# Attention of the later tiles with 64 and 8 keys of a head computed apart

## The chip, the cores and the metric

The kernel runs on one NeuronCore of one Trainium2 chip. The metric is device time in microseconds for one execution. The engines are named as the profile names them: PE (TensorE, matmuls) and PEld (its weight loads), DVE (VectorE), ACT (ScalarE), POOL (GpSimd) and SP (SyncE, which here only issues DMAs). Each engine works through its own list of instructions in order, and waits for the others through semaphores.

## The reference

Attention over keys and values that are averaged in groups of eight, followed by a two-layer network:

```python
B, H, S, D = 8, 8, 576, 64          # Sp = 576 // 8 = 72 pooled keys a head
k_p = k.reshape(B, H, Sp, 8, D).mean(axis=3)
v_p = v.reshape(B, H, Sp, 8, D).mean(axis=3)
scores = (1 / sqrt(D)) * q @ k_p.T   # per batch and head: 576 x 72
attn = softmax(scores)
x = (attn @ v_p)  -> (B*S, H*D) = (4608, 512)
h = x @ w_in      # 512 x 2048
out = (h * sigmoid(h)) @ w_out       # 2048 x 512
```

Inputs and outputs are float32; the products run in bfloat16 with float32 sums.

## The kernel before

The 4608 tokens are cut into nine tiles of 512. While the network's matmuls of tile t run, the attention of tile t + 1 is fitted in between. The network is computed by a seven-product scheme on halves (`unit`, line 678, and `out_product`, line 647), so that sums of inputs (`unit_x_sum`, line 476) and of hidden blocks (`hidden_sum`, line 574) stand ahead of the products.

The order on every engine is written out by hand. `tile_products` (line 615) walks through a string of items such as `a1` or `P5`; each is some steps long, 112 in an ordinary tile. A list of fillers is attached to step numbers by `at` and `late`, and `spread` (line 426) emits a filler behind its step. A filler's matmuls thus go between the network's, and its work on the other engines goes to the end of those engines' lists at that moment. Two fillers on the same engine run in the order of their steps.

Attention of one tile, for tiles 1 to 8, has these parts.

- Keys: `k_transpose` (line 202) or, for the first batches, `select_k` and `copy_k` put the pooled keys of batch b in `kz[b % 2]`. Four heads of 32 value pairs each lie on the 128 partitions (a is the group of four heads, c the even or odd half of D).
- Scores: `scores` (line 350) does one half of the tile's tokens (256) in one visit, at step 63 and again at 78. For each of four heads and two groups a matmul of 32 rows by 72 keys runs on its own quarter of the rows of PE. ACT takes the exponential of four 72 x 512 blocks (line 356).
- Sums: `denominators` (line 358) multiplies by ones, 72 rows by 32 columns, four column quarters; `reciprocals` (line 370) follows as exp(-ln).
- Values: `numerators` (line 401), 72 rows by 32 columns, into two banks a half; `x_half` (line 410) multiplies by the reciprocals on DVE and writes `xT`.

A tile that spans two batches has its matmuls cut in two at the border.

PSUM has eight banks: three go round under the tag `mm`, five under `at`. A tile takes the next in the round, so it waits for whoever used that bank last.

POOL's list in tile t, for t from 2 on: `behind_x_sums` (line 481), which copies one number of the last x sum and so waits for it; `pool_k` (line 194) for batch t + 1; the load of the next batch's first half of k (`load_one`, line 176); `pool_v` (line 197); the first half of v; the second halves (`load_rest`, line 182), which add onto the first halves and so wait until these have landed; and `load_q` at step 33. In tile 1 the loads come without the pooling, since batch 2 is pooled elsewhere. In tile 5 `load_q` consists of eight DMAs, since it is the last batch's; in tile 6 nothing is left to load.

The start is a stretch of its own: POOL issues the first loads of q and v, sets `shifts` and the identity, and then issues the loads of `w_in` (line 788).

Of the kernel before, what the change touches and what calls it, by code (L numbers as in the profile page):

```python
# [27 lines left out]
FP32 = mybir.dt.float32  # L28
# [8 lines left out]
def kernel(  # L37
# [62 lines left out]
    ones = singles.tile([SP, 32], BF16, name="ones")  # L100
# [18 lines left out]
    kz = [singles.tile([128, 2, 2, SP], BF16, name=f"kz{n}") for n in range(2)]  # L119
    kp = singles.tile([128, H, D], BF16, name="kp")  # L120
# [44 lines left out]
    PH = POOL // 2 * D  # L165

# [9 lines left out]
    def load_one(b, name):  # L176
        st = batches.setdefault(b, {})
        raw = raw_tile(f"{name}_raw3", H)
        nc.gpsimd.dma_start(out=raw, in_=source(b, name)[:, :, :PH])
        st[f"{name}_raw"] = raw  # L180

    def load_rest(b, name):
        nc.gpsimd.dma_start(
            out=batches[b][f"{name}_raw"], in_=source(b, name)[:, :, PH:],
            accum_op=ALU.add,
        )
# [9 lines left out]

    def pool_v(b):
        st = batches[b]
        st["vp"] = mid.tile([SP, H, D], BF16, tag="vp", name="vp")
        pool_rows(st["vp"], st["v_raw"])  # L200
# [91 lines left out]
    def select_v(b, a, tag="at"):  # L292
        st = batches[b]
        if a == 0:
            st["v_ps"] = ps_tile([128, H, D], FP32, tag, "v_ps")
            st["vp"] = mid.tile([SP, H, D], BF16, tag="vp", name="vp")
# [8 lines left out]

    def copy_v(b, a, copy=nc.vector.tensor_copy, heads=4):
        hs = slice(4 * a, 4 * a + heads)
        copy(out=batches[b]["vp"][:, hs, :], in_=batches[b]["v_ps"][:SP, hs, :])
# [14 lines left out]
    def es_tile():  # L323
        return mid.tile([SP, 4, 2 * NQ], BF16, tag="es", name="es")
# [25 lines left out]
    def scores(t, f):  # L350
        sc = [ps_tile([128, 512], FP32, "at", "sc_ps")[:SP] for s in range(4)]
        for g in range(2):
            score_matmuls(sc, t, f, g, g * NQ)
        es = half_state(t, f)["es"] = es_tile()
        for s in range(4):
            nc.scalar.activation(es[:, s, :], sc[s], func=AF.Exp, scale=score_scale)  # L356

    def denominators(t, f, den_ps=None):
# [3 lines left out]
        for s in range(4):  # L362
            nc.tensor.matmul(  # L363
                den_ps[32 * s : 32 * (s + 1), :],
                lhsT=ones, rhs=st["es"][:, s, :], start=True, stop=True,
            )
# [8 lines left out]
    def numerator_matmuls(nu, t, f, g, c, c0):  # L375
        for b, _, cs in half_units(t, f):
            for s in range(4):
                nc.tensor.matmul(  # L378
                    nu[32 * s : 32 * (s + 1), c0 + cs.start : c0 + cs.stop],
                    lhsT=batches[b]["vp"][:, 4 * g + s, c::2],  # L380
# [20 lines left out]
    def numerators(t, f, tags=("at", "at")):  # L401
        st = half_state(t, f)
        nu = []
        for c in range(2):
            nu.append(ps_tile([128, 512], FP32, tags[c], "nu_ps"))
            for g in range(2):
                numerator_matmuls(nu[c], t, f, g, c, g * NQ)
        st["nu"] = nu

    def x_half(t, f):  # L410
        st = half_state(t, f)
        for c in range(2):
            nc.vector.tensor_mul(  # L413
                out=xT[:, c::2, x_cols(t, f)],
                in0=st["nu"][c].rearrange("r (g n) -> r g n", g=2),
                in1=st["rec"].rearrange("r (g n) -> r g n", g=2),
            )
# [363 lines left out]
    nc.vector.memset(kp, 0.0)  # L781
    nc.gpsimd.memset(shifts, 0.0)
    make_identity(nc, ident, nomemset=True)

# [76 lines left out]
    for n in range(4):  # L861
        unit_weight_sum(0, 1, n)
    denominators(0, 1, den_ps)
# [28 lines left out]
    for t in range(NT):  # L892
        a = t + 1
        if t == 0:
# [17 lines left out]
            for j in range(2):  # L912
                at(60 + 2 * j, select_k, 1, j)
                at(60 + 2 * j, copy_k, 1, j, nc.scalar.copy)
            for i0, i1 in ((0, SA), (SA, SLOTS), (SLOTS, SLOTS + 1)):
                at(55, load_slots, nc.gpsimd, 2, "k", i0, i1)
# [8 lines left out]
            for j in range(2):  # L925
                at(83 + j, slot_sums, "v", j)
                at(100 + j, select_v, 1, j)
            at(101, copy_v, 1, 0, nc.scalar.copy, H)
# [5 lines left out]
            at(68, scores, 1, 0)  # L934
            at(79, scores, 1, 1)
            at(79, denominators, 1, 0)
            at(94, reciprocals, 1, 0)
            at(103, denominators, 1, 1)
            at(103, reciprocals, 1, 1)
            at(106, numerators, 1, 0)  # L940
            at(106, numerators, 1, 1, ("at", "mm"))
            for n in range(2):
                at(106, x_half, 1, n)
# [27 lines left out]
        if a < B:  # L971
            if t == 1:
                for j in range(2):
# [3 lines left out]
                    at(69, slot_sums, "v", j, halves=True)  # L977
                at(1, load_half_2, "v", 1)
                for j in range(2):
                    at(84, select_v, 2, j)  # L980
                at(84, copy_v, 2, 0, nc.scalar.copy, H)
# [5 lines left out]
            else:  # L987
# [10 lines left out]
                at(34, k_transpose, a)  # L998
        if t < NT - 1:
# [6 lines left out]
            late(63, scores, a, 0)  # L1006
            late(78, scores, a, 1)
            late(89, denominators, a, 0)
            late(89, reciprocals, a, 0)
            late(89, denominators, a, 1)  # L1010
            late(89, reciprocals, a, 1)
            for n in range(2):
                late(89, numerators, a, n)
            late(89, x_half, a, 0)
            late(91, moe_tables)
            late(95, x_half, a, 1)
# [32 lines left out]
```

## Time and profile before

| | |
|---|---|
| median of 3 runs | 273.1 us (272.92 to 273.17) |
| profiled execution: span | 272.3 us |
| ACT, exponential of the scores (line 356) | 64 x 590 ns |
| DVE, values times reciprocals (line 413) | 32 x 683 ns |
| POOL, pooling of k and v (lines 189 and 192) | 10 x 2357 ns, 10 x 1266 ns |
| POOL waiting for x sums (line 482) | 41.7 us in 6 waits |
| POOL waiting for the first half of v (line 183) | 14.6 us in 5 waits |
| POOL waiting for the first half of k (line 183) | 9.9 us in 5 waits |
| DMA | 37.72 MB, 139 GB/s mean |

The span runs from the first to the last instruction of the profiled execution; the measured time has a little more around it. A row of a timeline gives the start and the length in microseconds, the engine, the line of the kernel, the operation, what it writes and reads, its shape and how many follow each other; a bracket names the idle time before it and what ended it. Matmuls are pipelined: the length of one has its way through the array in it, and the distance from start to start is what a stream of them costs.

### The profile page before, as it was taken

To read this page: it belongs to the slowest core of one execution; us is meant where nothing else is said; L and a number is where in the kernel's file an instruction comes from. 1 tells how busy PE (TensorE), PEld (TensorE's weight loads), DVE (VectorE), ACT (ScalarE), POOL (GpSimd) and SP (SyncE) were. 2 spreads that over 40 slices of the span, in tenths; PEclk is the share of its full clock that TensorE was granted. 3 is DMA by queue.
4 is the path that set the end of the run, shared out by engine and by line. 5 is a ranking of instruction groups with operands and counts; after the bars stand their busy time and mean duration, and the time that the engine had idled before them with its cause. 6 is when DMAs were issued, how large, how long until landed. Compare 5 with 4: busy or idle time off the path is not lost.

```text
span 272.3 us, 7297 instructions
## 1 busy us (share of the span) xinstructions
PE 266.3 (98%) x2982; PEld 213.9 (79%) x2982; DVE 206.5 (76%) x363; ACT 194.1 (71%) x342; POOL 102.3 (38%) x111
## 2 busy tenths in 40 slices
PE   8999999999999999999999999999999999999994
PEld 4358644788888878887888788878888888788883
DVE  4759886879697949794979497849875987587861
ACT  1579776888858885888588858785878587867700
POOL 8655435672348413831383329383800000000000
PEclk9999999999999999999999999999999999999999
DMA  7999999586996796679657976799400140014004
GB/s 214 269 203 281 216 289 304 177 150 156 133 200 168 148 137 150 157 148 147 132 140 164 125 154 164 155 130 123 126 2 2 40 117 1 2 34 120 4 2 154
DMA packets 31585, 37.72 MB, mean 139 GB/s; under 512 B 10640, under 2 KB 22608, under 8 KB 31552
## 3 DMA queue, kind: packets, MB, share of 16 engines
q0 software_dynamic: 23904, 26.64, 52.4%
q1 hardware_dynamic: 7216, 9.97, 13.3%
q10 hardware_dynamic: 432, 0.66, 0.7%
q8 instruction: 23, 0.38, 0.6%
q14 instruction: 10, 0.08, 0.1%
HBM read 36.70 MB, written 9.44 MB: 169 GB/s over the span
## 4 chain that ended last, share of the span: by engine, by line
PE 92%; DMA 6%; POOL 0%; issue 0%; DVE 0%; POOLq 0%
PE u_psB L636 17%; PE o_psB L655 16%; PE u_psA L636 11%; PE u_psE L636 11%; PE o_psA L655 11%; PE o_psE L655 10%; PE o_ps L553 5%; PE sc_ps L331 3%; DMA raw<-in_v_dram 3%; DMA w_in_sb<-in_moe_w_in_dram 3%; PE nu_ps L378 3%; PE hp_ps L525 2%; PE den_ps L363 2%; POOL q_bf L127 0%; PE kz_ps L283 0%
## 5 line engine op out<-in xcount | busy, mean ns | idle before, releaser
L636 PEld LDWEIGHTS <-w_sum 128*128 128x128 bf16 x544 | 52.8, 98 | 7.5 <-issue 1.0
L655 PEld LDWEIGHTS <-h_sum 128*128 128x128 bf16 x512 | 48.6, 98 | 9.1 <-issue 2.6
L636 PEld LDWEIGHTS <-w_in_sb 128*128 128x128 bf16 x408 | 39.9, 98 | 5.0 <-issue 0.2
L655 PEld LDWEIGHTS <-h_T 128*128 128x128 bf16 x384 | 36.9, 98 | 5.3 <-issue 1.0
L636 PE MATMUL u_psA<-xT,w_in_sb 128*128 128x256 bf16 x272 | 40.5, 273 | 0.0
L636 PE MATMUL u_psB<-x_sum,w_sum 128*128 128x256 bf16 x272 | 40.2, 272 | 0.0
L356 ACT ACTIVATE es<-sc_ps 72x512 bf16<-72x512 f32 x64 | 32.7, 590 | 2.8 <-PE sc_ps L331 1.9
L655 PE MATMUL o_psB<-w_sum,h_sum 128*128 128x256 bf16 x256 | 33.0, 273 | 0.0
L655 PE MATMUL o_psA<-w_out_sb,h_T 128*128 128x256 bf16 x256 | 32.1, 273 | 0.0
L670 DVE TENSOR_TENSOR u_psE<-u_psB,p 128x512 f32<-128x512 f32 x34 | 23.7, 697 | 10.0 <-ACT p L668 6.1
L413 DVE TENSOR_TENSOR xT<-nu_ps,rec 128x512 bf16<-128x512 f32 x32 | 20.4, 683 | 12.6 <-ACT rec L373 10.5
L674 ACT ACTIVATE h_T<-u_psE 128x512 bf16<-128x512 f32 x34 | 20.3, 597 | 11.2 <-PE u_psE L636 10.4
L687 DVE TENSOR_TENSOR c<-u_psB,p 128x512 f32<-128x512 f32 x34 | 23.2, 681 | 3.1 <-PE u_psB L636 2.1
L665 DVE COPY u_psB<-u_psA 128x512 f32<-128x512 f32 x30 | 20.9, 698 | 5.5 <-PE u_psA L636 3.8
L674 ACT ACTIVATE h_T<-u_psB 128x512 bf16<-128x512 f32 x34 | 20.4, 599 | 5.9 <-PE u_psB L636 5.9
L674 ACT ACTIVATE h_T<-u_psA 128x512 bf16<-128x512 f32 x34 | 20.5, 602 | 4.7 <-PE u_psA L636 4.5
L189 POOL TENSOR_TENSOR raw<-raw 72x1024 f32<-72x1024 f32 x10 | 23.6, 2357 | 0.1
L668 ACT COPY p<-u_psE 128x512 f32<-128x512 f32 x34 | 20.0, 593 | 4.2 <-PE u_psE L636 4.0
L579 DVE TENSOR_TENSOR h_sum<-h_T 128x1024 bf16<-128x1024 bf16 x32 | 21.7, 680 | 0.2 <-ACT h_T L674 0.2
L674 ACT ACTIVATE h_T<-c 128x512 bf16<-128x512 f32 x34 | 21.7, 637 | 0.0
L579 DVE TENSOR_TENSOR h_sum<-h_T,h_sum 128x1024 bf16<-128x1024 bf16 (+1 forms) x24 | 20.7, 864 | 0.2
L636 PE MATMUL u_psB<-xT,w_sum 128*128 128x256 bf16 x136 | 20.6, 272 | 0.0
(89 smaller groups left out, 438.7 us busy)
## 6 DMA issues: line engine op xcount, KB each, us to landing
out_dram<-o_sb SPq DMA_DIRECT2D x128, 64.0 KB, 1.7
raw<-in_k_dram POOLq DMA_DIRECT2D x10, 576.0 KB, 8.2
raw<-in_v_dram POOLq DMA_DIRECT2D x10, 576.0 KB, 8.6
q_bf<-in_q_dram POOLq DMA_DIRECT2D x5, 576.0 KB, 11.3
w_in_sb<-in_moe_w_in_dram POOLq DMA_DIRECT2D x8, 256.0 KB, 8.6
w_out_sb<-in_moe_w_out_dram POOLq DMA_DIRECT2D x4, 512.0 KB, 10.7
raw<-in_v_dram POOLq DMA_DIRECT2D x2, 768.0 KB, 10.4
raw<-in_k_dram POOLq DMA_DIRECT2D x2, 768.0 KB, 10.0
```

The costliest lines, as they stand in the source:

```text
L189: nc.gpsimd.tensor_add(out=raw[:, :, : 2 * D], in0=raw[:, :, : 2 * D], in1=raw[:, :, 2 * D :])
L356: nc.scalar.activation(es[:, s, :], sc[s], func=AF.Exp, scale=score_scale)
L413: nc.vector.tensor_mul(out=xT[:, c::2, x_cols(t, f)], in0=st["nu"][c].rearrange("r (g n) -> r g n", g=2), in1=st["rec"].rearrange("r (g n) ...
L553: nc.tensor.matmul(ps["m", m], lhsT=h_T[:, g, m * 128 : (m + 1) * 128], rhs=w_out_sb[:, g, :], start=(g == 0), stop=(g == KG - 1),)
L579: nc.vector.tensor_tensor(out=h_sum[n][:, k0:k1, :], in0=get(a), in1=get(b), op=op)
L636: nc.tensor.matmul(ps[y, BANK[n]][:, u, :], lhsT=w[:, kk, 128 * u : 128 * (u + 1)], rhs=x[:, kk, :], start=n in (1, 5) and u == 0 and kk == 0,
L655: nc.tensor.matmul(o_bank(n, c), lhsT=left(n, kt, c), rhs=w[:, kt, :], start=n in (1, 5) and kt == 0 and c == 0, stop=kt == KQ - 1, skip_g ...
L665: (acopy if t == 0 or (t == 1 and y in (0, 1)) else vcopy)(ps[y, "B"], ps[y, "A"])
L668: acopy(f32[y], ps[y, "E"])
L670: tt(out=ps[y, "E"], in0=ps[y, "B"], in1=f32[y], op=add)
L674: nc.scalar.activation(h_T[:, g : g + 2, j * NQ : (j + 1) * NQ], src, func=AF.Silu)
L687: tt(out=c22, in0=ps[y, "B"], in1=f32[y], op=add)
```

## The change

From tile 1 on, the 72 keys of a head are treated as 64 and 8. `scores(t)` handles the whole tile in one visit: the first 64 keys of the heads of both groups on tiles of 32 rows by 64 columns, eight at a time, with 512 columns each; the last eight keys of four heads go together in one matmul of 128 rows by 32 columns, whose weights `kzr` are block-diagonal (four heads by eight keys, zero elsewhere). The exponentials then are four of 128 x 512 and one of 128 x 256. `sum_matmuls` and `value_matmuls` use tiles of 64 rows by 32 columns for the 64 keys, and add the last eight keys by masked ones `ones_r` and block-diagonal values `vr`.

`spread_keys` makes `kzr` by four products of the last eight keys with a mask, `spread_values` makes `vr` by two; both on POOL unless told otherwise. The values lie in a tile of 128 partitions with a fifth column block for the last keys. For batches 0, 1 and 2 `pick_v` builds it by matmuls (batch 0 also keeps the old form `vp0` for tile 0); for later ones v is loaded in that layout: the first 64 keys in two DMAs for each half, the last eight keys in four DMAs from SP. `pool_v` gets three more additions and calls `spread_values`. Masks are made at the start.

```diff
     def load_one(b, name):
+        if name == "v":
+            st["v_raw"] = big.tile([128, 4, PH], FP32, tag="v_raw3", name="v_raw")
+            st["r_raw"] = big.tile([128, 2 * PH], FP32, tag="r_raw3", name="r_raw")
+            load_v_half(b, 0)
+            for n in range(4):
+                hs = slice(4 * (n // 2), 4 * (n // 2) + 4)
+                nc.sync.dma_start(
+                    out=st["r_raw"][32 * n : 32 * (n + 1)],
+                    in_=v[b].rearrange("h (sp p) d -> h sp (p d)", p=POOL)[hs, KM:],
+                )
+            return
...
+    def load_v_half(b, half):
+        for g in range(2):
+            nc.gpsimd.dma_start(
+                out=batches[b]["v_raw"][KM * g : KM * (g + 1)],
+                in_=source(b, "v")[:KM, 4 * g : 4 * (g + 1), PH * half : PH * (half + 1)],
+                **(dict(accum_op=ALU.add) if half else {}),
+            )
...
     def pool_v(b):
         st = batches[b]
-        st["vp"] = mid.tile([SP, H, D], BF16, tag="vp", name="vp")
-        pool_rows(st["vp"], st["v_raw"])
+        vp = value_tile(b)
+        pool_rows(vp[:, :4], st["v_raw"])
+        raw = st["r_raw"]
+        for w in (PH, PH // 2, PH // 4):
+            nc.gpsimd.tensor_add(
+                out=vp[:, 4] if w == D else raw[:, :w], in0=raw[:, :w], in1=raw[:, w : 2 * w]
+            )
+        spread_values(b)
...
+    def spread_keys(b, eng=nc.gpsimd):
+        for a in range(2):
+            for c in range(2):
+                eng.tensor_tensor(
+                    out=kzr[b % 2][:, a, c].rearrange("r (s k) -> r s k", s=4),
+                    in0=kz[b % 2][:, a, c : c + 1, KM:].broadcast_to([128, 4, SP - KM]),
+                    in1=mask_k.unsqueeze(2).broadcast_to([128, 4, SP - KM]), op=ALU.mult,
+                )
...
+    def pick_v(b):
...
+        for g in range(2):
+            for s in range(4):
...
+                    nc.tensor.matmul(
+                        ps[KM * g : KM * (g + 1), s, :], lhsT=shifts[:, x : x + KM],
+                        rhs=v5[:, i], start=(s == 0 and j == 0), stop=(j == len(segs) - 1),
+                        skip_group_check=True,
+                    )
+        for n in range(4):
+            for s in range(4):
+                h = 4 * (n // 2) + s
+                nc.tensor.matmul(
+                    ps[32 * n : 32 * (n + 1), 4, :], lhsT=pick_r[:, h],
+                    rhs=v5[:, (SP * h + KM) // 128], start=False, stop=(s == 3),
+                    skip_group_check=True,
+                )
+        nc.scalar.copy(value_tile(b), ps)
...
+    def scores(t):
+        st = att[t] = {}
+        sc = [ps_tile([128, 512], FP32, "at", "sc_ps") for _ in range(4)]
+        scr = ps_tile([128, 512], FP32, "at", "sr_ps")
+        for n, (b, us, cs) in enumerate(tile_units(t)):
+            for c in range(2):
+                for s in range(4):
+                    rows = slice(32 * s, 32 * (s + 1))
+                    for g in range(2):
+                        nc.tensor.matmul(
+                            sc[s][KM * g : KM * (g + 1), cs],
+                            lhsT=kz[b % 2][rows, g, c, :KM],
+                            rhs=qT[rows, g, us, :, c],
+                            start=(n == 0 and c == 0), stop=(c == 1), skip_group_check=True,
+                        )
         for c in range(2):
...
+                nc.tensor.matmul(
+                    scr[32 * n : 32 * (n + 1), cs],
+                    lhsT=kzr[b % 2][:, g, c, :], rhs=qT[:, g, us, :, c],
+                    start=(first and c == 0), stop=(c == 1), skip_group_check=True,
+                )
+        for s in range(4):
+            nc.scalar.activation(st["es"][:, s, :], sc[s], func=AF.Exp, scale=score_scale)
+        nc.scalar.activation(st["er"], scr[:, :NQ], func=AF.Exp, scale=score_scale)
...
+        for s, g, rows in lanes:
+            one(s, g, slice(0, NTT), ones[rows], st["es"][rows, s, :], start=True, stop=False)
+        for f in range(2):
+            cols = slice(f * NQ, (f + 1) * NQ)
+            for s, g, rows in lanes:
+                one(s, g, cols, ones_r[rows, 4 * f + s], st["er"][rows], start=False, stop=True)
...
+    def value_matmuls(t, tags=("at", "at", "at", "mm")):
+        nu = st["nu"] = [
+            [ps_tile([128, 2, NQ], FP32, tags[2 * g + f], "nu_ps") for f in range(2)]
+            for g in range(2)
+        ]
...
     nc.gpsimd.memset(shifts, 0.0)
     make_identity(nc, ident, nomemset=True)
+    nc.gpsimd.memset(pick_r, 0.0)
+    for h in range(H):
+        r, s0 = (SP * h + KM) % 128, (SP - KM) * (h % 4)
+        nc.gpsimd.tensor_copy(
+            out=pick_r[:, h, s0 : s0 + SP - KM], in_=ident[:, r : r + SP - KM]
+        )
+    nc.gpsimd.memset(mask_q, 1.0)
+    for base, sign in ((0, 1), (SP - KM - 1, -1)):
+        nc.gpsimd.affine_select(
...
@@ tile 0: attention of tile 1
+            at(46, spread_keys, 0)
+            at(46, pick_v, 0)
+            at(47, spread_values, 0)
+            at(63, spread_keys, 1, nc.vector)
...
+            at(70, scores, 1)
+            at(87, sums, 1)
+            at(106, value_matmuls, 1)
+            for g in range(2):
+                at(106, x_part, 1, g)
@@ tile 1
+                at(32, spread_keys, 2)
+                at(76, pick_v, 2)
+                at(77, spread_values, 2)
@@ tiles 2 to 6
                     at(33, load_q, a + 1)
                 at(34, k_transpose, a)
+                at(35, spread_keys, a)
@@ tiles 1 to 7
-            late(63, scores, a, 0)
-            late(78, scores, a, 1)
-            late(89, denominators, a, 0)
-            late(89, reciprocals, a, 0)
-            late(89, denominators, a, 1)
-            late(89, reciprocals, a, 1)
-            for n in range(2):
-                late(89, numerators, a, n)
-            late(89, x_half, a, 0)
-            late(91, moe_tables)
-            late(95, x_half, a, 1)
+            late(63, scores, a)
+            late(87, sums_and_values, a)
+            late(88, x_part, a, 0)
+            late(88, moe_tables)
+            late(95, x_part, a, 1)
```

## The prediction

> **What bounds the kernel now.** I read the page first: span, engine shares, the row of granted clock.
>
> ```profile
> span 272.3 us, 7297 instructions
> PE 266.3 (98%) x2982; PEld 213.9 (79%) x2982; DVE 206.5 (76%) x363; ACT 194.1 (71%) x342; POOL 102.3 (38%) x111
> PEclk9999999999999999999999999999999999999999
> ```
>
> TensorE works in every slice at full clock, so whatever TensorE no longer does, or newly waits for, shows in the time nearly one for one. POOL at 38% looks like an engine with room. But a mean says nothing of when its work gets done, so I read two timelines over one steady pass (t = 4, which prepares tile 5). TensorE first: start, length, operation, count.
>
> ```profile
> 144.39 0.60 PE L636 MATMUL u_psB<-xT,w_sum 128*128 128x256 bf16 x4
> 144.83 1.91 PE L655 MATMUL o_psA<-w_out_sb,h_T 128*128 128x256 bf16 x16
> 146.57 0.60 PE L636 MATMUL u_psB<-xT,w_sum 128*128 128x256 bf16 x4
> 147.10 0.65 PE L331 MATMUL sc_ps<-qT,kz 32*72 32x256 bf16 x16
> 147.68 1.05 PE L655 MATMUL o_psA<-w_out_sb,h_T 128*128 128x256 bf16 x8
> ...
> 153.80 0.60 PE L655 MATMUL o_psB<-w_sum,h_sum 128*128 128x256 bf16 x4
> 154.33 0.61 PE L363 MATMUL den_ps<-es,ones 72*32 72x512 bf16 x8
> 154.77 1.07 PE L378 MATMUL nu_ps<-es,vp 72*32 72x256 bf16 x48
> ```
>
> Four 256-column matmuls take 0.44 us start to start: 109 ns each. A change of lane shape costs 0.09 us (153.80 + 0.44 = 154.24, den_ps starts at 154.33). Scores start at 147.10. Now POOL in the same pass:
>
> ```profile
> 133.82 0.19 POOL L482 COPY gate<-x_sum 128x1 bf16<-128x1 bf16 x1 [10.03 <-DVE x_sum L479]
> 138.85 2.38 POOL L189 TENSOR_TENSOR raw<-raw 72x1024 f32<-72x1024 f32 x1
> 141.31 1.27 POOL L192 TENSOR_TENSOR vp<-raw 72x512 bf16<-72x512 f32 x1
> 143.05 0.83 POOL L179 DMA_DIRECT2D raw<-in_v_dram  x1 [0.47 <-POOL vp L192]
> 150.16 1.40 POOL L183 DMA_DIRECT2D raw<-in_v_dram  x1 [4.15 <-DMA raw<-in_v_dram]
> 150.99 1.32 POOL L145 DMA_DIRECT2D q_bf<-in_q_dram  x1
> ```
>
> POOL starts its pass only when the tile's x sums exist (gate), and the second half of v waits 4.15 us in POOL's queue until the first half has landed. The queue is through at about 152, five us after the scores began. Today nobody waits for that, since it only loads the next batch. The pass t = 5 is worse, because eight q loads follow and the last waits for v's second half:
>
> ```profile
> 177.92 5.25 POOL L138 DMA_DIRECT2D q_bf<-in_q_dram  x7
> 186.22 0.66 POOL L138 DMA_DIRECT2D q_bf<-in_q_dram  x1 [3.06 <-DMA raw<-in_v_dram]
> ```
>
> **The change part by part.** The sum is made against the profiled execution, span 272.3; the median of the runs is 273.1, so 0.8 lies around it.
>
> *Columns on TensorE.* Before, per tile: scores 32 x 256 columns on four lanes, sums 8 x 512 on four, values 32 x 256 on four: 5120 column times. After: scores 16 x 512 on eight lanes plus 8 x 256 on four, sums 8 x 512 and 16 x 256 on eight, values 32 x 256 on eight plus 8 x 256 on four: 4096. The 1024 less are 0.44 us at 109 ns per 256. Changes of lane shape: six before (two score visits, one of sums and values), six after (32x64, 128x32, back; 64x32, 32x128, back): nothing. Eight tiles: -3.5 us. No row shows eight lanes at once. If they ran like four, 1024 (scores) + 1024 (sums) + 1024 (values) column times come back and the gain turns into a loss of 0.9 per tile; four lanes start 3 ns apart, so eight fit into 109 ns, and I take eight.
>
> *pick_v.* Six 64-column v_ps matmuls take 0.18 us, so select_v's twelve 0.36. pick_v has 12 on two lanes and 16 on four: 0.18 + 0.12 + three shape changes 0.27 = 0.57. It runs for three batches in place of two select_v (batch 0 is now selected twice): +1.0.
>
> *kzr, the decisive part.* The last eight keys' scores need kzr, and spread_keys makes it with four small products. For batches 2 to 6 they are put in POOL's queue behind the second half of v, and for 3 to 6 behind the q load too (step 35 against 33). TensorE executes in order, so the rest scores, and all MoE matmuls behind them, wait for POOL. Ready time at t = 4: pool_v becomes 128x512 (1.26), 128x256 (0.73) twice, 128x128 (0.45), 64 wide (0.32, read on from those), and two spread products of 128 (0.45 each): 4.4 where it was 3.7, ending at 143.5; the 0.47 wait behind it is used up. First halves of v are now two issues, 143.5 and 144.15 (0.65 apart, as the seven q issues in 5.25 stand). From issue to the second half's issue took 7.1 (143.05 to 150.16), so the two second halves go at 150.6 and 151.25, q at 151.9, the products start at 152.65 (0.73, the shortest L145 issue). Three of them must be done: 0.25 each, between the 0.19 of a 128x1 copy and 0.45 of 128x128; with 0.1 for the signal 153.5. TensorE stands there at 147.10 + 0.44 + 0.09 = 147.6. Stall 5.9 us. The same at t = 2: 94.34 + 2.9 against 92.3: 5.0. t = 3: 121.64 + 3.45 against 120.0: 5.1. t = 1 (batch 2, not behind q): second half at 68.15, + 2.15 = 70.3, against 64.5: 5.8. t = 5: the last q now goes about 187.4, + 1.6 = 189.0 against 175.3: 13.7. t = 6 loads nothing more, so POOL reaches the products 9.5 us behind the gate and TensorE needs them 13.8 behind it: none. t = 7 has none to make; batch 1's run on DVE. The gate hangs on x sums, hence on TensorE, so a late pass doesn't let POOL catch up; the stall returns in each. Sum +35.5. Bounds: issues of 0.55 and products of 0.19 take 1.2 off each stall (-6); issues as long as their rows (1.40, 1.32) and products of 0.45 add 2 (+10).
>
> *The clock after a stall.* In the timeline the first nine warm matmuls and three later ones:
>
> ```profile
> 1.19 4.02 PE L759 MATMUL warm_ps<-warm 128*128 128x512 bf16 x9 [1.19 <-DVE warm L778]
> 7.36 0.82 PE L759 MATMUL warm_ps<-warm 128*128 128x512 bf16 x3
> ```
>
> Nine take 4.02 and three 0.82: about 0.43 us each against 0.22, so TensorE starts at half pace for some 4 us. At the end it stops at 268.5, and by stretches (the sixth figure group is the granted clock) the clock falls behind it:
>
> ```profile
> 268.50:271.60 3.10, 0.02 (x1) 0.00 (x0) 0.42 (x1) 0.00 (x0) 0.00 (x0) 1.00 0.66 239
> 271.60:272.30 0.70, 0.00 (x0) 0.00 (x0) 0.00 (x0) 0.00 (x0) 0.00 (x0) 0.57 0.00 0
> ```
>
> So 3.1 us of idle end in a lower clock. All five stalls are longer. Each then loses half of 4 us: 2.0, five times +10. Bounds: 0 if a wait in the middle doesn't count as such an idle time, 17 if half pace lasts 7 us.
> The Trainium skill (TensorE: Matmul & The Clock Gate, Part 1) has the clock at half or full only, dropping after an idle window of about 3.4 us and returning after a busy one, with windows that run freely. By that a 5 us stall holds a whole idle window only half of the time; estimated, 3.4 drops of 2.5 us: +8.7 where I have 10, and the sum would end near 316.5. The two rows above agree with it in kind.
>
> *Smaller things.* POOL's masks (about 2.5 us by the 0.45 memset, 0.19 copies and 0.29 select) stand ahead of the w_in loads; three issues of 0.72 behind them reach 10.9, and the fourth waited until 10.93 anyway for v. Take +0.5 (0 to 2.5). Tile 1's x products start when all four value banks are complete, where the first half was ready earlier: +0.8 (0 to 1.3). The fourth value bank follows o_psA, whose copy (L700, 0.69) has only just begun: 0.2 in the two passes without a stall, +0.4. Exp: eight of 0.59 become four and one of about 0.37; ScalarE isn't the limit, nothing. New DVE memsets lie in its 2.4 us wait for k; without that cover 0.4. Four r_raw loads per pass wait in SP's queue for POOL; the stores behind them come some 10 us later: nothing, but their 0.25 MB lands beside v's and could lengthen its 6 to 7 us (in the upper bound).
>
> Sum: -3.5 + 1.0 + 35.5 + 10 + 0.5 + 0.8 + 0.4 = +44.7: span 317.0, time 317.8.
>
> **The rivals.** *Stall without the clock* (25%): the clock keeps full in the waits. For it: one fall in the trace, at the very end, with no instruction left to come. 308.
> *POOL slower still* (13%): its issues cost their full rows and r_raw crowds v. Speaks for it that rows overlap their successors, so that 0.65 and 0.73 may be too short behind a busy ring. 327.
> *No stall, not slower* (4%): kzr is there in time. Then only -3.5 + 2.7 remains: 272.3. It would need v's first half to land about 5 us sooner (1 to 2 us, not 6 to 7), and in t = 5 the second half as well; below that the wait begins at once. Rows of five passes (waits of 14.6 us in all for this landing) speak against it.
> *Eight lanes work as four*: 0.44 + 0.87 worse in each of eight tiles, +10.5 on top: 328; 3%.
>
> **How the numbers follow.** Forecast 55% at 317.8. The range must take in 308 with shorter issues (303) and 327: 303 to 328. A no-change result is under 0.2% of the time (0.55 us), about what a measurement of this kernel can tell. Only the no-stall case can be there or below: faster 0.025, same 0.015; slower 0.96.
>
> **What would show it.** After: the chain of waits has POOL's kzr products and the v and q loads; the weight load or matmul of the rest scores waits for POOL kzr in five passes, 5 to 6 us and once 13 to 14; TensorE's share falls to about 85%; slices with PEclk below 9 follow each stall. Passes t = 6 and 7 are shorter by some 0.3 us: that is the gain. Wrong, if kzr finds TensorE not yet at the rest scores; if MoE matmuls behind a stall stay at 109 ns; if a sums or values visit isn't shorter than den_ps and nu_ps were (1.44 us).

## The result, and the profile after

The changed kernel took 317.6 us (median of four executions, 315.6 to 318.7) against 273.1 for the kernel before (272.9 to 273.4): a ratio of 1.162, with a 95% interval of 1.157 to 1.166. The forecast was 317.8. The profiled execution had a span of 317.0 us and a time of 318.7.

From the page of the kernel after: the span, the engines' shares, the row of granted clock, the chain that ended last by engine, and the group of the rest scores (busy time, mean, and then idle time before them with what ended most of it).

```profile
span 317.0 us, 7920 instructions
...
PE 278.7 (88%) x3234; PEld 219.3 (69%) x3234; DVE 208.9 (66%) x377; ACT 181.9 (57%) x319; POOL 121.4 (38%) x190
...
PEclk9999999995899879995999699985899999999999
...
PE 45%; DMA 23%; POOL 17%; issue 9%; SPq 2%; DVE 2%; POOLq 0%; DVEq 0%
...
L520 PE MATMUL sr_ps<-qT,kzr 128*32 128x256 bf16 (+3 forms) x88 | 7.3, 298 | 31.0 <-POOL kzr L258 30.9
```

From the first matmul of tile 1 to that of tile 8 the seven passes took 28.2, 27.7, 27.6, 27.7, 27.6, 27.7 and 27.6 us before the change, and now take 40.6, 34.2, 34.2, 33.7, 40.9, 27.3 and 27.1.

Before, every figure in the clock row was a 9 and TensorE was busy for 98% of the span. Now there are five dents in the row, and POOL and DMA hold 40% of the chain, although POOL's share is still 38%. The view of waits (who waits for whom: us in all, times, longest) names the places:

```profile
PE sr_ps L520 <- POOL kzr L258: 30.9, 5, 10.7
...
POOL v_raw L202 <- DMA v_raw<-in_v_dram: 10.4, 8, 2.0
POOL raw L212 <- DMA raw<-in_k_dram: 9.1, 1, 9.1
```

TensorE waits for kzr in five passes, and POOL, ahead of kzr in its queue, waits for landings. The timelines of the pass t = 3 show it in order. TensorE first, from the scores to the next tile:

```profile
139.66 0.66 PE L507 MATMUL sc_ps<-qT,kz 32*64 32x256 bf16 x32
140.25 0.29 PE L520 MATMUL sr_ps<-qT,kzr 128*32 128x256 bf16 x1
144.93 0.99 PE L520 MATMUL sr_ps<-qT,kzr 128*32 128x256 bf16 x7 [4.39 <-POOL kzr L258]
145.86 1.89 PE L843 MATMUL o_psA<-w_out_sb,h_T 128*128 128x256 bf16 x8
147.54 2.83 PE L843 MATMUL o_psE<-w_sum,h_sum 128*128 128x256 bf16 x16
...
159.69 0.49 PE L824 MATMUL u_psA<-xT,w_in_sb 128*128 128x256 bf16 x3
```

The tile spans two batches. The first rest score reads the kzr of the earlier one, which was made a pass before, and so reaches the array; the second starts 4.68 us later. The eight o_psA matmuls behind the wait need 1.68 us from start to start (145.86 to 147.54), 0.21 each where 0.11 is full pace. And POOL in the same pass:

```profile
126.37 0.19 POOL L670 COPY gate<-x_sum 128x1 bf16<-128x1 bf16 x1 [15.23 <-DVE x_sum L667]
...
136.53 1.27 POOL L202 DMA_DIRECT2D v_raw<-in_v_dram  x2
137.79 1.50 POOL L212 DMA_DIRECT2D raw<-in_k_dram  x1
141.33 1.03 POOL L202 DMA_DIRECT2D v_raw<-in_v_dram  x1 [2.04 <-DMA v_raw<-in_v_dram]
142.86 1.00 POOL L202 DMA_DIRECT2D v_raw<-in_v_dram  x1 [0.51 <-DMA v_raw<-in_v_dram]
143.49 1.12 POOL L151 DMA_DIRECT2D q_bf<-in_q_dram  x1
144.24 1.21 POOL L258 TENSOR_TENSOR kzr<-kz,mask_k 128x32 bf16<-128x32 bf16 x4
```

That is the queue of the prediction: the first halves of v are issued 10.2 us after the gate, the second halves wait for their landing, then q, then the products, 0.20 us from one to the next. In t = 5 the q issues, and a wait among them, stand in between as well:

```profile
210.66 1.00 POOL L202 DMA_DIRECT2D v_raw<-in_v_dram  x1 [1.30 <-DMA v_raw<-in_v_dram]
211.28 3.76 POOL L144 DMA_DIRECT2D q_bf<-in_q_dram  x5
...
218.17 0.66 POOL L144 DMA_DIRECT2D q_bf<-in_q_dram  x1 [0.68 <-DMA v_raw<-in_v_dram]
218.85 0.83 POOL L258 TENSOR_TENSOR kzr<-kz,mask_k 128x32 bf16<-128x32 bf16 x4
```

The granted clock around the stall of t = 3, by stretches (after the time and the five engines' busy times with counts comes the clock, then DMA):

```profile
140.25:142.50 2.25, 0.29 (x9) 0.09 (x1) 2.25 (x4) 2.22 (x4) 1.03 (x1) 1.00 0.74 133
142.60:144.90 2.30, 0.00 (x0) 0.00 (x0) 1.16 (x1) 1.14 (x3) 2.04 (x6) 0.50 1.10 169
145.00:149.40 4.40, 4.40 (x24) 2.79 (x25) 0.00 (x0) 0.38 (x1) 0.45 (x3) 0.50 1.19 192
149.40:153.00 3.60, 3.60 (x41) 3.01 (x46) 0.70 (x1) 0.59 (x1) 0.00 (x0) 1.00 0.53 101
```

The clock is at half from 2.3 us after the start of the last matmul before the wait (140.25 us), and stays there for 4.5 us of work.

### The profile page after: what moved, and what is told of

Read it like the earlier page. It is cut to its first block, busy times and chain, and to the rows that moved or that the text cites. A ratio compares the mean times of both kernels' runs of the same rounds, so it can differ in the third digit from the quotient of the medians.

```text
span 317.0 us, 7920 instructions
## 1 busy us (share of the span) xinstructions
PE 278.7 (88%) x3234; PEld 219.3 (69%) x3234; DVE 208.9 (66%) x377; ACT 181.9 (57%) x319; POOL 121.4 (38%) x190
## 4 chain that ended last, share of the span: by engine, by line
PE 45%; DMA 23%; POOL 17%; issue 9%; SPq 2%; DVE 2%; POOLq 0%; DVEq 0%
PE o_psB L843 11%; DMA v_raw<-in_v_dram 9%; PE o_psE L843 8%; DMA raw<-in_k_dram 7%; PE o_psA L843 7%; PE u_psB L824 6%; PE u_psA L824 4%; PE u_psE L824 4%; DMA w_in_sb<-in_moe_w_in_dram 3%; DMA q_bf<-in_q_dram 3%; POOL v_raw L202 2%; SPq L702 2%; POOL w_in_sb L993 2%; POOL kzr L258 1%; POOL raw L218 1%
## 5 line engine op out<-in xcount | busy, mean ns | idle before, releaser
L843 PEld LDWEIGHTS <-h_sum 128*128 128x128 bf16 x512 | 53.0, 105 | 10.4 <-issue 0.4
L843 PEld LDWEIGHTS <-h_T 128*128 128x128 bf16 x384 | 38.7, 102 | 7.1 <-issue 1.1
L858 DVE TENSOR_TENSOR o_psE<-o_psB,p 128x512 f32<-128x512 f32 x7 | 4.9, 699 | 55.2 <-PE o_psB L843 55.2
L843 PE MATMUL o_psA<-w_out_sb,h_T 128*128 128x256 bf16 x256 | 36.1, 295 | 0.0
L520 PE MATMUL sr_ps<-qT,kzr 128*32 128x256 bf16 (+3 forms) x88 | 7.3, 298 | 31.0 <-POOL kzr L258 30.9
L843 PE MATMUL o_psB<-w_sum,h_sum 128*128 128x256 bf16 x256 | 30.9, 273 | 0.0
L670 POOL COPY gate<-x_sum 128x1 bf16<-128x1 bf16 x6 | 1.1, 189 | 72.4 <-DVE x_sum L667 72.4
L520 PEld LDWEIGHTS <-kzr 128*32 128x32 bf16 x88 | 2.8, 98 | 35.4 <-POOL kzr L258 33.2
L202 POOL DMA_DIRECT2D v_raw<-in_v_dram x20 | 18.2, 1008 | 10.4 <-DMA v_raw<-in_v_dram 10.4
L843 PE MATMUL o_psE<-w_sum,h_sum 128*128 128x256 bf16 x128 | 22.0, 343 | 0.0
```

Of the source, the lines that this page charges most:

```text
L202: nc.gpsimd.dma_start(out=batches[b]["v_raw"][KM * g : KM * (g + 1)], in_=source(b, "v")[:KM, 4 * g : 4 * (g + 1), PH * half : PH * (half ...
L520: nc.tensor.matmul(scr[32 * n : 32 * (n + 1), cs], lhsT=kzr[b % 2][:, g, c, :], rhs=qT[:, g, us, :, c], start=(first and c == 0), stop=(c ...
L843: nc.tensor.matmul(o_bank(n, c), lhsT=left(n, kt, c), rhs=w[:, kt, :], start=n in (1, 5) and kt == 0 and c == 0, stop=kt == KQ - 1, skip_g ...
L858: tt(out=ps[y, "E"], in0=ps[y, "B"], in1=f32[y], op=add)
```

## The experiments

My theory was that the order in POOL's queue costs the time, twice over: TensorE waits for kzr, and then runs at half pace for a while. The rivals: the waits alone cost it, POOL itself is too slow, or another part of the change costs as much.

**kzr on DVE.**

```diff
-                at(32, spread_keys, 2)
+                at(38, spread_keys, 2, nc.vector)
...
-                at(35, spread_keys, a)
+                at(38, spread_keys, a, nc.vector)
```

> The kernel after, with the four products that make kzr for batches 2 to 7 given to DVE (behind the copies that make kz) instead of POOL; nothing else differs. Theory (order in POOL's queue): the waits of the rest scores for kzr go, 32.3 us by the gaps of the profile after, and with them the stretches at half clock, some 13 us by the matmuls counted in them; 317.6 - 32.3 - 13 = 272.3, and 271 to 274 with DVE's four more products of 0.18 us a pass. The row of granted clock shows 9 throughout and the chain of waits has no kzr. Rival (the change costs elsewhere too, for instance eight lanes that run as four, or a fourth value bank that comes late): the stalls go, but the time stays at 278 to 283. Rival (TensorE waits for another thing at the same place, the copies of kz or q): the wait keeps its length under another name, over 310.

Measured: 275.5 us (274.9 to 278.6) against 273.0, a ratio of 1.012 (1.007 to 1.017). The wait for kzr is gone, and the clock row is all 9. Four small instructions a pass, given to the other engine, are worth 42 us. The eight lanes are not the cost: passes 2 to 6 take 27.25 to 27.29 us where they took 27.64 to 27.67. But the time lies 3 us above the 272.3 that waits and clock should have left. Waits of TensorE in this run:

```profile
PE hp_ps L713 <- DMA w_in_sb<-in_moe_w_in_dram: 0.8, 1, 0.8
PE o_psE L843 <- ACT es L528: 0.6, 1, 0.6
...
PE nu_ps L573 <- POOL vr L248: 0.5, 1, 0.5
```

The last two are both in tile 1, which took 31.1 us from its first matmul to that of tile 2, where it was 28.2 before. On DVE the slot sums of batch 2's values (line 323) now stand ahead of the hidden sums (line 767) that the o_psE matmuls need:

```profile
66.19 0.55 DVE L323 TENSOR_TENSOR raw<-raw 128x384 f32<-128x384 f32 x1
...
67.71 0.69 DVE L767 TENSOR_TENSOR h_sum<-h_T 128x1024 bf16<-128x1024 bf16 x1
```

The change had moved these sums from step 69 to 62, and `spread_values` of batch 2 stands on POOL behind k's second half. The view names ACT for the wait of 0.6 us, but the hidden sum ended last, at 68.40 us, and the matmuls start at 68.45. I had priced neither piece.

**kzr on POOL, but ahead of the loads.**

```diff
-                    at(5, load_rest, 3, n)
-                at(33, load_q, 3)
+                    at(36, load_rest, 3, n)
+                at(36, load_q, 3)
...
-                    at(3, load_rest, a + 1, "k")
-                    at(4, load_rest, a + 1, "v")
-                    at(33, load_q, a + 1)
                 at(34, k_transpose, a)
                 at(35, spread_keys, a)
+                if a + 1 < B:
+                    for n in "kv":
+                        at(36, load_rest, a + 1, n)
+                    at(36, load_q, a + 1)
```

> The kernel after, with kzr's products still on POOL but the second halves of k and v and the q load put behind them (step 36) in tiles 1 to 5. Theory (what stands ahead of the products costs, not the engine that makes them): the products run as soon as kz is there, about 2 us before TensorE asks for them, so no stall and 271.5 to 274. Rival (POOL as such is too slow or too late, since its products take 0.23 to 1.41 us in the profile after and its pass starts with the x sums): 2 to 4 us of stall stay in each of five passes, 285 to 300. Possible new cost: k's second half goes out later, and the next pass's pooling finds it missing; then POOL runs late in the next pass but its products still stand ahead of the loads, under 2 us in all.

Measured: 276.7 us (274.5 to 279.3), ratio 1.017 (1.011 to 1.022). No wait for kzr is left either: in t = 2 the products run 10.8 us behind the gate, and TensorE gets to them at 13.9. So POOL as an engine is good enough, and what stood ahead of the products was the cost. The time is above my range. In the profile tile 1 takes 31.4 us, with the same late pieces as in the run with DVE; that profiled execution, at 274.5, was the shortest of the four, and what made the others longer is not shown.

**TensorE kept busy in the waits.** Matmuls that nobody reads stand ahead of the rest scores; kzr comes no sooner.

```diff
+        for _ in range({2: 34, 3: 16, 4: 16, 5: 15, 6: 46}.get(t, 0)):
+            nc.tensor.matmul(scr, lhsT=warm[:, :128], rhs=warm, start=True, stop=True)
```

> The kernel after, with matmuls that nobody reads (512 columns, 0.216 us each: 34, 16, 16, 15 and 46 of them in passes 1 to 5) set ahead of the rest scores, so that TensorE works through most of each wait for kzr; kzr comes no sooner. Theory (13 us of the loss are matmuls at half clock behind the waits): the clock keeps full, and the time falls to 317.6 - 13 = 304.6, 303 to 306.5, though TensorE does 27 us more work. Rival (the clock in the record follows the waits but costs little; the loss of 45 us lies in waits alone): 316 to 319.

Measured: 308.7 us (307.9 to 312.0), ratio 1.133 (1.126 to 1.139): 8.9 us less than the kernel after, with 127 more matmuls. That is neither the rival's 317 nor my 304.6. TensorE in the pass t = 3:

```profile
135.59 3.63 PE L514 MATMUL sr_ps<-warm 128*128 128x512 bf16 x16
139.15 0.29 PE L522 MATMUL sr_ps<-qT,kzr 128*32 128x256 bf16 x1
140.74 0.86 PE L522 MATMUL sr_ps<-qT,kzr 128*32 128x256 bf16 x7 [1.31 <-POOL kzr L258]
141.53 1.05 PE L845 MATMUL o_psA<-w_out_sb,h_T 128*128 128x256 bf16 x8
```

The eight o_psA matmuls take 1.05 us with the last one's way through the array, where they took 1.89: 0.11 each again. From the end of the wait to the next tile's first matmul the passes 1 to 4 take 13.69, 12.91, 12.91 and 12.89 us; in the kernel after it was 16.38, 14.85, 14.76 and 15.18, and 15.13 in pass 5. With 12.9 for pass 5 the half clock cost 2.7 + 1.9 + 1.9 + 2.3 + 2.2 = 11.0 us. The run shows less than that since its waits ended later, counted from the gate (by 0.5, -0.2, 0.5, 0.9 and 1.8 us, 3.5 in all), and since in pass 5 of the profiled execution 2.5 us of idle time were left, in which the clock fell once more (1.2). 11.0 - 3.5 - 1.2 = 6.3, against 6.7 between the two spans.

**The q load alone behind kzr.**

```diff
-                at(33, load_q, 3)
+                at(36, load_q, 3)
...
-                    at(33, load_q, a + 1)
+                    at(36, load_q, a + 1)
```

> The kernel after, with only the q load moved behind kzr's products in tiles 1 to 5; the second halves of k and v stay ahead. Theory: in pass 5 the last seven of the eight q issues (211.28 to 218.85 in the profile after) leave the path, so its stall falls from 11.0 to about 4 us; in passes 2 to 4 one issue of 0.65 each; pass 1 keeps its 8.3. Together 9 us of stall, and up to 2 of half clock: 306 to 309. Rival (the products wait for v's landing alone and q's issues cost nothing, as they fit into that wait): 316 to 318.

Measured: 309.1 us (308.0 to 311.1), ratio 1.133 (1.128 to 1.138). POOL in the pass t = 5:

```profile
207.13 1.00 POOL L202 DMA_DIRECT2D v_raw<-in_v_dram  x1 [1.12 <-DMA v_raw<-in_v_dram]
207.78 1.24 POOL L258 TENSOR_TENSOR kzr<-kz,mask_k 128x32 bf16<-128x32 bf16 x4
208.97 4.81 POOL L144 DMA_DIRECT2D q_bf<-in_q_dram  x7
```

The stall of t = 5 is 3.7 us where it was 11.0, so q's issues were on the path there, as predicted. The other four stalls are 7.7, 3.7, 4.5 and 3.7 us, up to 0.9 less than before. In the first of them q stood behind the products already, and it is 0.6 shorter all the same, so one issue's worth in the others can't be told from the scatter between two profiles.

**kzr made twice.**

```diff
                 at(32, spread_keys, 2)
+                at(32, spread_keys, 2)
...
                 at(35, spread_keys, a)
+                at(35, spread_keys, a)
```

> The kernel after, with the four products that make kzr issued twice on POOL in passes 1 to 6. Theory (they stand on the path of five passes, at 0.20 us each from start to start): 0.8 us a pass, 321.6, 320.5 to 323.5. Rival (the wait ends with something else, such as q, and kzr only happens to come last): 316 to 319.

Measured: 321.0 us (319.8 to 323.0), ratio 1.175 (1.171 to 1.178): 3.3 us more than the kernel after. Eight products follow each other at 0.20 us, so four more are 0.8 a pass and 4.0 in all; the five stalls of the profile add up to 35.8 us where they were 32.3. The products are on the path.

**The loads of v's last keys later.** Four loads a pass on SP go from step 1 to step 90.

```diff
-            for n in range(4):
-                hs = slice(4 * (n // 2), 4 * (n // 2) + 4)
-                nc.sync.dma_start(
-                    out=st["r_raw"][32 * n : 32 * (n + 1)],
...
+                at(90, load_r, 3)
...
+                    at(90, load_r, a + 1)
```

> The kernel after, with the four loads of v's last keys moved on SP from step 1 to step 90 of each pass, away from the landing of k's and v's first halves. Theory A (they take no part in the stalls; v's first half lands 4 to 5 us after its issue as it is): 316 to 319. Theory B (they crowd the first halves, most of all in pass 1, where k's took 12.4 us in the profile after and 9.4 in the one before): pass 1's stall falls from 8.3 to 5 or 6 us and the others by 0.3 to 0.5: 312 to 314. I hold B for pass 1 and A for the others: 313 to 316.

Measured: 318.4 us (317.7 to 319.4), ratio 1.164 (1.161 to 1.166), and pass 1 keeps its stall (8.26 us). What I held for pass 1 was wrong: these loads take no part.

**v of batch 3 later in tile 1.** This asks for the reason of the one stall that was mis-sized by much.

```diff
-                for n in "kv":
-                    at(4, load_one, 3, n)
-                for n in "kv":
-                    at(5, load_rest, 3, n)
+                at(4, load_one, 3, "k")
+                at(5, load_rest, 3, "k")
+                at(36, load_one, 3, "v")
+                at(37, load_rest, 3, "v")
```

> The kernel after, with both halves of v of batch 3 in tile 1 moved behind kzr's products and the q load; passes 2 to 5 as they are. The stall of pass 1 was predicted at 5.8 us and was 8.3, since the first half of k took 12.4 us from issue to the issue that waits for it, where it was 9.4 before the change; the four loads of v's last keys had no part in that. Theory A (v's two loads, right behind k's on the same ring, draw k's landing out): k takes 9 us or less, the stall falls to 3 or 4 us, with the two second issues of v (0.65 each) gone from the path too: 311 to 313.5. Theory B (k's landing is slow for another reason): k still takes 12 us, the stall loses the two issues alone, 7.0 us: 315 to 318.

Measured: 321.8 us (319.3 to 323.4), ratio 1.176 (1.169 to 1.183): slower, which neither theory had. In the kernel after, k's issue at 58.65 is answered at 71.07, 12.4 us later:

```profile
58.65 2.04 POOL L197 DMA_DIRECT2D raw<-in_k_dram  x1
59.56 2.41 POOL L202 DMA_DIRECT2D v_raw<-in_v_dram  x2
71.07 1.43 POOL L212 DMA_DIRECT2D raw<-in_k_dram  x1 [9.10 <-DMA raw<-in_k_dram]
```

Without v beside it:

```profile
60.55 2.04 POOL L197 DMA_DIRECT2D raw<-in_k_dram  x1
70.56 1.39 POOL L212 DMA_DIRECT2D raw<-in_k_dram  x1 [7.98 <-DMA raw<-in_k_dram]
...
84.85 2.10 POOL L202 DMA_DIRECT2D v_raw<-in_v_dram  x2 [8.81 <-DMA v_raw<-in_v_dram]
86.38 1.34 POOL L248 TENSOR_TENSOR vr<-vp,mask_v 128x128 bf16<-128x128 bf16 x2
```

and on TensorE

```profile
87.44 0.75 PE L573 MATMUL nu_ps<-er,vr 32*128 32x256 bf16 x11 [4.09 <-POOL vr L248]
```

k takes 10.0 us, and the wait for kzr falls to 4.0 us, with 1.4 more behind it: v's loads draw k's landing out by some 2.4. (In the other twelve profiles of the new form, with v behind k, this load of k landed 11.5 to 12.6 us after its issue, and here after 9.7.) But v's second half now stands ahead of `spread_values` of batch 2, and TensorE waits 4.3 us for vr: the same fault at another place. Tile 1 takes 42.2 us where it took 40.6; of the 3.0 us between the two spans the rest lies ahead of tile 1, in the start. Before the change k took 9.4 us with v beside it, so why v in its new form costs k more is still open.

**Tile 1 mended, kzr on DVE.**

```diff
-                    at(62, slot_sums, "v", j, halves=True)
+                    at(69, slot_sums, "v", j, halves=True)
...
-                at(76, pick_v, 2)
-                at(77, spread_values, 2)
+                at(79, pick_v, 2)
+                at(80, spread_values, 2, nc.vector)
```

> The run before with kzr on DVE (275.5, 274.9 to 278.6) and three fillers of tile 1 moved: the slot sums of batch 2's values behind the hidden sums on DVE (step 69 instead of 62), pick_v of batch 2 three steps later, and spread_values of batch 2 on DVE instead of POOL, where it stood behind k's second half. Theory (the stall of tile 1 covered two other late pieces, which show once it is gone: the hidden sums with 0.79 and 0.32 us, vr with 0.62 and 0.23): 2.0 less, 273.5 (273 to 274.5), and, since vr no longer waits for a landing, runs that lie close together. Rival (the 3 us above 272.3 lie in the start, which came up to 1 us later from profile to profile, or are scatter of the chip): it stays at 275 to 276 and keeps the scatter.

Measured: tile 1 takes 29.1 us instead of 31.1, as expected, and the profiled execution 273.1. But twelve executions go from 273.1 to 279.9 (median 274.8; ratio 1.004, 1.002 to 1.007), the longest at a mean clock of 0.985 to 0.987. So tile 1 was not the reason for the scatter.

**The same three moves, with kzr left on POOL.** The edit is that of the run above, made in the kernel after.

> The kernel after with only tile 1's three fillers moved (slot sums of batch 2's values, pick_v and spread_values of batch 2), kzr still on POOL behind the loads. With kzr on DVE these moves took 2 us out of tile 1 in the profiles. Theory (in the kernel after the wait for kzr covers those 2 us): nothing, 316 to 319. Rival (they add to the wait): 315 to 316.

Measured: 318.8 us (316.0 to 319.6), ratio 1.165 (1.161 to 1.169). The same moves give nothing here: the wait for kzr covers the late pieces.

**All moves that promised something.** Beside the above: POOL's masks behind its loads of w_in, the sums and values of tiles 1 to 7 at step 89, and the values of tile 1 at step 103.

```diff
-    nc.gpsimd.memset(pick_r, 0.0)
...
-    nc.gpsimd.memset(mask_q, 1.0)
...
             # loads of w_in
+    nc.gpsimd.memset(pick_r, 0.0)
...
+    nc.gpsimd.memset(mask_q, 1.0)
...
+            at(45, value_masks)
...
-            at(106, value_matmuls, 1)
+            at(103, value_matmuls, 1)
...
-            late(87, sums_and_values, a)
+            late(89, sums_and_values, a)
```

> The run with kzr on DVE and tile 1 mended, with three more moves: POOL's masks behind the loads of w_in at the start (0.6 to 1.1 us of w_in's landing in the profiles), sums and values two steps later in tiles 1 to 7 (step 89, as before the change, so that the fourth value bank is free: 0.19 us a pass), and the values of tile 1 at step 103 instead of 106 (x sums 0.6 us earlier). Theory: 273.5 - 0.8 - 1.3 - 0.6 = 270.8, 270 to 272, faster than the kernel before by 0.8% (0.4 to 1.1). Rival (what is saved at one place is waited for at the next): 272.5 to 273.5, the same.

Measured: 272.9 us (272.4 to 274.6) against 273.35, ratio 0.9985 (0.9970 to 0.9999). The executions lie closer together, but the gain is 0.15% where I expected 0.8%. Passes 2 to 5 take 27.3 to 27.5 us where they took 27.3 with step 87. The visit of sums and values takes 1.32 to 1.46 us, where it mostly took 1.52 to 1.54 with step 87, so most of the wait for the fourth bank goes, but between o_psA and o_psB a wait of 0.15 us is back that the kernel before had as well:

```profile
125.55 1.04 PE L843 MATMUL o_psA<-w_out_sb,h_T 128*128 128x256 bf16 x8
126.57 0.60 PE L843 MATMUL o_psB<-w_sum,h_sum 128*128 128x256 bf16 x4
127.10 0.41 PE L536 MATMUL den_ps<-es,ones 64*32 64x512 bf16 x8
```

Eight matmuls of 0.109 us would have ended at 126.42. At step 87 the visit of sums and values lies exactly there and covers it.

**The masks alone** (that run with step 87 and step 106 put back).

> The run with kzr on DVE and tile 1 mended (274.8, 273.1 to 279.9, the long ones at a granted clock of 0.985 to 0.994), with one more move: POOL's masks behind its loads of w_in, and DVE's mask products from them at step 45. Theory (the masks put w_in off by 3 us, TensorE waits for it at the start, 1.0 us in the profile, and in some executions long enough for the clock to fall): no execution above 274.5, clock 1.0 in all, median 272.5 to 273.3. Rival (the scatter comes from pass 1 or from the sums two steps earlier, which the run with all moves had also changed back): the scatter stays, some executions above 276 at a lower clock.

Measured: 272.31 us (272.15 to 272.64) against 273.26, ratio 0.9968 (0.9956 to 0.9980). It is 0.3% faster than the kernel before. From the page:

```profile
span 270.2 us, 7908 instructions
...
PEclk9999999999999999999999999999999999999999
```

The mean clock is 0.998 to 1.0 in all six executions. In the run with kzr on DVE the masks and the first w_in load stood like this on POOL:

```profile
6.46 0.31 POOL L975 MEMSET pick_r<- 128x256 bf16 x1
...
9.13 5.74 POOL L993 DMA_DIRECT2D w_in_sb<-in_moe_w_in_dram  x8
```

and here

```profile
6.83 0.74 POOL L980 DMA_DIRECT2D w_in_sb<-in_moe_w_in_dram  x1
```

TensorE's wait for w_in at the start, 1.3 us in the kernel after and 0.8 in the run with DVE, is no longer in the profile. None of the longest executions of the run before was profiled, so that this wait let their clock fall is not shown. Two other profiles show that it can: with v's last keys later, and with tile 1's moves and kzr on POOL, TensorE stood idle for 1.3 and 1.2 us before products with w_in, the clock was at half for the next 3.4 us, and tile 1 began at 54.1 and 52.9 us, where it began at 49.7 to 52.6 in the other profiles with the masks ahead of w_in. The clock is at most part of it: estimated from a mean of 0.986 over 277 us, it costs about 4 of the up to 7 us.

**Values of tile 1 earlier** (step 103 instead of 106).

> The run before this one with the values of tile 1 at step 103 instead of 106; that is the run with all moves (272.9) but with the sums and values of tiles 1 to 7 at step 87, as the change has them. Theory (step 89 brought back a wait of 0.15 us a pass at o_psB that the change had taken away, and one of 0.26, which cost as much as the 0.19 us for the fourth bank): 272.3, 271.7 to 272.7, faster than before by 0.4% (0.2 to 0.6). Rival (step 89 was as good): 272.7 to 273.1.

Measured: 272.4 us (271.7 to 273.9), ratio 0.9968 (0.9954 to 0.9981): no different from the run above. Both ratios lie below that of the run with step 89, but the intervals overlap (0.9970 to 0.9999 there); in the profiles passes 2 to 5 take 109.1 us in both and 109.5 with step 89. That fits the reading of step 89 and does not prove it. Step 103 gives nothing because vr comes no sooner:

```profile
47.35 0.28 PE L573 MATMUL nu_ps<-er,vr 32*128 32x256 bf16 x5 [0.65 <-DVE vr L248]
```

## Why the prediction was right, step by step

The mechanism was right, and so were its terms in the main. That the time came out within 0.2 us is luck: the stalls were put 3.2 us too long, and terms that were put too small or left out made up for it.

*Columns (-3.5).* Right in size. When the wait at the rest scores, what follows it and the half clock (below) are taken off, passes 2 to 7 are each 0.37 to 0.45 us shorter than before, and the last tile 0.5. Eight lanes run at once: eight score matmuls start 3 ns apart, and the next eight 0.11 to 0.14 us after them. The term was 0.44 a pass, less the fourth bank. The scores take 0.94 us where the two visits took 1.16 to 1.19. The visit of sums and values got longer, 1.52 to 1.54 us where it was 1.43 to 1.44: by the prediction's last sign that would speak against eight lanes, but the fourth bank's wait lies in it, about 0.19 us in every pass and not in two. What made up for it lies outside the visits, where a pass is some 0.25 us shorter: 0.15 of that is a wait between o_psA and o_psB, which the visit two steps earlier covers and which I had not seen; the rest I can't place.

*The stalls (+35.5).* The sum was 3.2 us too large, and its parts were further off. The waits are counted from the start of the last matmul before to the start of the next; the view of waits counts idle time alone and has 30.9.

| pass | predicted | wait at the rest scores | what differed |
|---|---|---|---|
| 1 | 5.8 | 8.3 | k's landing 12.4 us, not 9.4 |
| 2 | 5.0 | 4.6 | |
| 3 | 5.1 | 4.7 | |
| 4 | 5.9 | 3.7 | v's first half landed sooner |
| 5 | 13.7 | 11.0 | the same, and shorter waits among the q issues |
| sum | 35.5 | 32.3 | |

The term "from issue to the second half's issue took 7.1" is the one that was off: with v in two loads of 256 KB the first was there after 4.8 us (136.53 to 141.33). Against that the second load had a wait of its own, so that 1.5 us lay between the two second issues instead of 0.65. The first issue 9.7 us behind the gate (measured 9.6 to 10.2), the q issue (0.75 where I had 0.73) and the products (0.20 where I had 0.25) were right. A term that I left out: the remaining rest scores come in late and a change of shape later, 0.4 us a stall, some 2.2 in all, by the passes with TensorE kept busy (12.9 us from the wait to the next tile) against an undisturbed one (12.5).

*The clock (+10).* Right, 11.0 by the same passes. The rival without it fell. By the clock's records the half stretches are 6.8, 10.2 or 13.7 us long, multiples of 3.4, and the clock falls 2.2 to 2.7 us after the last matmul's start in t = 2 to 5, and 4.3 us after it in t = 1. The Trainium skill (TensorE: Matmul & The Clock Gate, Part 1) has a fall only where an idle window of about 3.4 us fits in whole, from which I had estimated 3.4 falls; here all five waits had one, the shortest of 3.7 us, and four of the falls came sooner than 3.4 us. Five more profiles have kzr behind these loads (q later, kzr twice, v's last keys later, tile 1's moves, v of batch 3 later). With them it is 30 waits for kzr, 3.4 to 10.8 us of idle time, and all 30 had a fall, from 2.0 to 5.4 us after the last matmul's start; some came up to 1.2 us after TensorE had resumed.

*Smaller terms.* The x products of tile 1: predicted +0.8, measured 0.77. pick_v took 0.66 us where I had 0.57. The masks at the start: +0.5 was too little; in the profiles TensorE's wait for w_in grew by 1.0, and I had not seen that such a wait can bring a fall of the clock. The start as a whole came 1.3 us later. The later `spread_values` and the earlier slot sums of tile 1, 2 us, were not in the working; the stall covered them, so the sum did not suffer.

All in all, from the profiles: 32.3 + 2.2 + 11.0 for the five stalls, +1.3 for the start, +0.9 for the rest of tile 1, -2.9 for the shorter passes and the tail: 44.8, and the spans differ by 44.7.

*The rivals.* Eight lanes as four fell with the passes of 27.3 us. POOL slower still: not in sum, and r_raw has no part in it. No stall: kzr found TensorE waiting in five passes. What of "what would show it" failed: the waits are 3.7 to 8.3 us and once 11.0, not 5 to 6 and once 13 to 14; TensorE's share is 88% and not 85%, since half-clock matmuls count as busy; and the visit of sums and values did not get shorter (above).

## What to carry to other kernels

Before an instruction is put on an engine with a low share, read what stands ahead of it in that engine's queue in the pass where it is needed: a DMA issue that waits for another landing holds up everything behind it, however short. A large stall covers smaller faults of the same change, so when it is mended, look at the pass again before the rest is called free. And price a gap of a few us on TensorE with the half clock behind it: here every one with at least 3.4 us of idle time had it.

## What I had not expected of the hardware

- In the waits for kzr the clock fell as little as 2.0 us after the last matmul's start. Idle times of 3.4 us and more all had a fall, and one of 2.5 us in the run with TensorE kept busy. Of the shorter ones, 1.18 and 1.29 us at the start had a fall in two profiles, while 1.20, 1.31 and 1.59 us in others had none, so the length alone did not decide. In the kernel after, a fall cost 1.9 to 2.7 us of work whether the wait was 3.7 or 11.0 us long.
- k's first half in tile 1 took 12.4 us with v's two loads right behind it and 10.0 without; before the change it took 9.4 with one load of v behind it.
- A wait of about 1 us for a load at the start went with executions up to 7 us apart; with the masks moved behind the loads the executions of a run lay 0.5 to 2.2 us apart (three runs). That the wait itself spreads them is not shown.
